# A fused attention and two-MoE kernel: a rewritten order of the instructions of a head pair, 128-row maxima for head 0, and second buffers for the rests of k and q

## The chip, the cores and the metric

The kernel runs on one core of a Trainium2 chip. The metric is the device time of one execution in microseconds (us). The engines are named as the profile names them: PE is TensorE's matmul pipe and PEld its weight loads, DVE is VectorE, ACT is ScalarE, POOL is GpSimd, and SP is SyncE, which only issues DMAs here.

## The reference

Attention over 16 heads (2 batches of 8) with 1152 keys, a head size of 64, and queries averaged in pairs (576 queries per head); then a gated MoE layer; then four experts mixed by `domain_probs`.

```python
q_pool = q.reshape(B, H, S // 2, 2, D).mean(axis=3)
scores = scale * np.matmul(q_pool, k.transpose(0, 1, 3, 2))
attn = np.exp(scores - np.max(scores, axis=-1, keepdims=True))
x = np.matmul(attn / attn.sum(-1, keepdims=True), v)
x = (x @ w_a * (x @ w_b)) @ w_out          # 1152x512 by 512x1536
out = sum(p[:, e] * (np.maximum(x @ w1[e], 0) @ w2[e]) for e in range(4))
```

## The kernel before

**Precision.** Each factor that must be exact is split into a high part (fp32r) and a rest: kh and kl for k, qh and ql for q. The rests of k, of q and the sum qs of the two queries live in the pool `lo`.

**Stages.** Attention takes the first 290 us or so, and what follows it (the two MoE layers) the rest. The heads come in eight pairs; the two heads of a pair lie in the upper and the lower 64 partitions of kq, kh, kl, qh and ql.

**One head.** For each of 9 key tiles a step `qk` writes scores: two matmuls of At (kh over kl) with QHt (qh twice), line 527, and two of Bt (kh and a row of ones) with QLt (ql and the row of negative maxima), line 532. ACT takes the exponential (`e`, line 537; PS has two score buffers). A step `pv` multiplies by V (line 542, four passes). After nine of them `evac` copies the result out on ACT, and the next head's first `pv` writes into the same PSUM banks. The tiles At, Bt, QHt and QLt exist once for even and once for odd heads; they are filled by SBUF-to-SBUF copies that SP issues: `da` (two, from kh and kl), `db` (from kh), `dh` (two, from qh), `dl` (from ql), and the row of maxima (`rm`, `rw`, from mr).

**Maxima.** While pair p is scored, the maxima of pair p+1 are found: 27 steps `mx`, each one matmul of kh with QB (block-diagonal qh, line 417) into one of two PSUM buffers, and one reduction on DVE (line 432). A third `mx` must wait for the first one's reduction. QB is filled by `qb`, two DMAs.

**What sets the order.** It is written out by hand. `FIRST` is the list for heads 0 and 1, `PROG` for a pair (18 steps `qk`: nine for the even head, nine for the odd). Each engine and SP takes its instructions strictly in this order. Other tokens: `k`, `qs`, `qh`, `ql`, `klo0` to `klo2` make the parts of a later pair (casts on ACT, differences on DVE, line 332 for klo); `lq`, `lk0` to `lk2`, `ldf` load q, thirds of k, and v; `nr`, `nb`, `n` normalise the previous pair; `w` is one step of splitting a weight; the last step of a split issues the load of the next weight block (`stg`, 1 MB, line 143). `klo0` writes kl, which `da` of the same pair's odd head reads.

**Head 0** is scored in two column parts, C0 = 256 queries (token `A`, part `a` of the pv) and the other 320 (`C`, `c`), so that it can begin before all of q is there. Its maxima are taken per 128 queries (tiles 0 to 4): tiles 0 to 2 ahead of the token list, tiles 3 and 4 as six tokens `x`; `r1` turns those of the second part into a row. All of them use the upper 64 rows alone (kh with qh). `warm` puts matmuls of zeros in front.

Of the kernel before, what the change touches and what calls it, by code (L numbers as in the profile page):

```python
# [34 lines left out]
STOP = None  # L35
KR = 3
KN = S // KR
WARM = (8, 2, 2)
NE = 8
NORM = ("nr", "nb", "n", "n", "n", "n")  # L40
C0 = 256
C1 = SQ - C0
FIRST = """
A kh1
A x qh1 kl1 x a dh1 ql1 da1 lv1 a x x
A
A x x a a zq a r1 db1 qs a y y k
C
C klo0 y a y a y c y c klo2 y y qh
# [13 lines left out]
""".split()  # L63
FIRST_ONLY = set("A C a c x y r1 R1 E1 E2 qh1 kh1 kl1 ql1 da1 dh1 db1 lv1 zq".split())
PROG = """
qk mx da dh dl db rw
qk mx pv mx
qk mx pv mx pv klo0 lq
qk mx pv mx evac
mx qk mx klo1  # L70
mx qk n pv mx pv ql mx pv
mx qk mx klo2 lk0
mx qk w mx ldf nr pv lk1
mx qk nb mx pv lk2
mx qk mx da dh dl db
mx qk mx pv
mx qk mx
qk mx qs pv n mx pv w pv evac
qk mx k
qk w qh pv ldf n n qb pv rm pv w  # L80
qk w pv
qk
qk n pv n w
""".split()
ENG = {"qs": "V", "qh": "A", "k": "A", "ql": "V", "klo0": "V", "klo1": "V", "klo2": "V", "mult": "V", "xhi": "A", "xlo": "V"}
F64_TINY_BITS = 2.0 ** -15
# [4 lines left out]
def kernel(  # L91
# [139 lines left out]
    with tc.manual_schedule():  # L231
        att = ExitStack()
        kq_p = att.enter_context(tc.tile_pool(name="kq", bufs=2))
        pair_p = att.enter_context(tc.tile_pool(name="pair", bufs=2))
        lo_p = att.enter_context(tc.tile_pool(name="lo", bufs=1))
        b_p = att.enter_context(tc.tile_pool(name="b", bufs=1))
        e_p = att.enter_context(tc.tile_pool(name="e", bufs=NE))
        m_p = att.enter_context(tc.tile_pool(name="m", bufs=2))
# [9 lines left out]
        def psum(kind, base, n, count):  # L248
            i = turn[kind]
            turn[kind] = (i + 1) % count  # L250
            return PS[:, base + i * n:base + (i + 1) * n, :]
# [10 lines left out]
        def rows(i):  # L262
            return slice(64 * i, 64 * i + 64)

        def fill_consts(i, e):
            fill = e.memset
            one = 64 - 64 * i
            fill(QLt[i][rows(1 - i), :].bitcast(F32), 0.0)
            fill(Bt[i][rows(1 - i), :].bitcast(F32), 0.0)
            fill(Bt[i][one:one + 1, :].bitcast(F32), 1.0)  # L270
# [17 lines left out]
        emitted = set()  # L288
# [20 lines left out]
        def load_q(p):  # L309
            q_t[p] = q_p.tile([128, S], F32, tag="q", name="q")  # L310
            nc.sync.dma_start(out=q_t[p], in_=kq[p, :, S:])
# [49 lines left out]
        def own_qh(i, e, cs=slice(0, SQ)):  # L361
            cast(e, QHt[i][rows(i), cs], qs_t[0][rows(i), cs])

        def own_ql(i, e, cs=slice(0, SQ)):
            e.tensor_tensor(
                out=QLt[i][rows(i), cs], in0=qs_t[0][rows(i), cs],
                in1=QHt[i][rows(i), cs].bitcast(F32), op=ALU.subtract,
            )

        def own_kh(i, ks):  # L370
            cast(nc.scalar, At[i][rows(i), ks], kq_t[0][rows(i), ks])
# [37 lines left out]
        def max_mm(out, h, qi, r):  # L409
            p, i = divmod(h, 2)  # L410
            ks = slice(r * KN, (r + 1) * KN)
            if p > 0:
                lhs, rhs = QB[:, qi, :], kh_t[p][:, ks]
            else:
                part = rows(0) if i == 0 else slice(0, 128)
                lhs, rhs = QHt[i][part, qi * 128:min(SQ, (qi + 1) * 128)], At[i][part, ks]
            nc.tensor.matmul(out=out[:lhs.shape[1]], lhsT=lhs, rhs=rhs, start=True, stop=True)  # L417

        def max_slot(h, qi):
            p, i = divmod(h, 2)  # L420
            if p not in m_t:
                m_t[p] = m_p.tile([128, 10, KR], F32, tag="m", name="m")
            return m_t[p][:n_q(h, qi), qi + 5 * i, :]

        def n_q(h, qi):
            return min(128, SQ - 128 * qi) if h < 2 else 128

        def max_step(h, i):
            qi, r = divmod(i, KR)
            mx = psum("mx", 2, 1, 2)[:, 0, :KN]  # L430
            max_mm(mx, h, qi, r)
            nc.vector.tensor_reduce(  # L432
                out=max_slot(h, qi)[:, r:r + 1], in_=mx[:n_q(h, qi)], axis=AX.X, op=ALU.max
            )

        def max_wide(h, qi, base):
            for r in range(KR):
                max_mm(PS[:, base + r, :KN], h, qi, r)
            nc.vector.tensor_reduce(
                out=max_slot(h, qi)[:, 0:1], in_=PS[:, base:base + KR, :KN], axis=AX.XY, op=ALU.max  # L440
            )

        def max_col(p, c, n=KR, parts=128):
            if p not in mc_t:
                mc_t[p] = m_p.tile([128, 10], F32R, tag="mc", name="mc")
            nc.vector.tensor_reduce(
                out=mc_t[p][:parts, c], in_=m_t[p][:parts, c, :n], axis=AX.X, op=ALU.max
            )
# [16 lines left out]
        def row_direct(c):  # L465
            cs, tiles = ((slice(0, C0), range(2)), (slice(C0, SQ), range(2, 5)))[c]
            mx = PS[:, 3, :] if c == 0 else psum("mx", 2, 1, 2)[:, 0, :]
            for qi in tiles:
                n, at = n_q(0, qi), 128 * (qi - tiles[0])
                nc.tensor.matmul(  # L470
                    out=mx[0:1, at:at + n], lhsT=mc_t[0][:n, qi:qi + 1], rhs=nid[:n, :n],
                    start=True, stop=True,
                )
            nc.scalar.activation(
                out=QLt[0][64:65, cs], in_=mx[0:1, :cs.stop - cs.start], func=AF.Copy
            )
# [144 lines left out]
        def warm(n, bank=0):  # L621
            for _ in range(n):
                nc.tensor.matmul(out=PS[:, bank, :], lhsT=Z[:, :128], rhs=Z, start=True, stop=True)
# [5 lines left out]
        nc.vector.memset(Z.bitcast(F32), 0.0)  # L629
        warm(WARM[0])  # L630
        fill_consts(0, nc.gpsimd)
# [30 lines left out]
        own_ql(0, nc.gpsimd, c1)  # L662
        warm(WARM[1], 4)
        row_direct(0)
        max_wide(0, 2, 0)
        load_q(1)
        for r in range(KR):
            load_k(1, r)
# [17 lines left out]
        count = dict.fromkeys("ACacxy", 0)  # L686

        def first(tok):
            n = count.get(tok, 0)
            if tok in count:  # L690
                count[tok] += 1
            if tok in "AC":
                assert tok == "A" or "r1" in emitted
                qk_half(tok == "C", n)
                emitted.update((tok, t) for t in (2 * n, 2 * n + 1))
                if tok == "C" and n == KT // 2:
                    emitted.add(("qk", 0, KT - 1))
            elif tok in "ac":
                assert (tok.upper(), n) in emitted
                pv_half(tok == "c", n)  # L700
                pv_at[0] += tok == "c"
            elif tok == "x":
                assert n < 2 * KR
                max_step(0, 3 * KR + n)
            elif tok == "r1":
                assert count["x"] == 2 * KR
                max_col(0, slice(2, 3), 1)
                max_col(0, slice(3, 4))
                max_col(0, slice(4, 5), KR, 64)
                row_direct(1)  # L710
                emitted.add("r1")
            elif tok == "y":
                assert n < 5 * KR and {"dh1", "da1"} <= emitted
                max_step(1, n)
            elif tok == "R1":
                assert count["y"] == 5 * KR
                max_col(0, slice(5, 9))
                max_col(0, slice(9, 10), KR, 64)
                row_one()
                emitted.add(("row", 1))  # L720
            elif tok in ("E1", "E2"):
                assert count["ac"[tok == "E2"]] == KT
                evac_half(tok == "E2")
                emitted.add(("evac", 0) if tok == "E2" else "E1")
            else:
                need = {"kl1": "kh1", "ql1": "qh1", "dh1": "qh1", "db1": "kh1", "da1": "kl1"}
                assert tok not in need or need[tok] in emitted
                {
                    "qs1": lambda: own_qs(1, nc.gpsimd),
                    "qh1": lambda: own_qh(1, nc.scalar),  # L730
                    "kh1": lambda: own_kh(1, slice(0, S)),
                    "kl1": lambda: [own_klo(1, r, nc.gpsimd) for r in range(KR)],
                    "ql1": lambda: own_ql(1, nc.gpsimd),
                    "da1": lambda: own_put_kl(1, slice(0, S)),
                    "dh1": lambda: own_put_qh(1),
                    "db1": lambda: put(Bt[1][rows(1), :], At[1][rows(1), :]),
                    "lv1": lambda: [fill_v(1, nc.gpsimd), load_v(1)],
                    "zq": lambda: nc.gpsimd.memset(QB.bitcast(F32), 0.0),
                }[tok]()
                emitted.add(tok)  # L740

        for h in range(1, min(NHX, NH)):
# [3 lines left out]
            for tok in FIRST if h == 1 else PROG[half:] if h % 2 else PROG[:half]:  # L746
# [45 lines left out]
                elif tok in ("nr", "nb", "n"):  # L792
                    i = norm_at[0]
                    pr, i = divmod(i, 6)
# [125 lines left out]
        w = W.pop(("ab", 0))  # L920
# [14 lines left out]
        for f in range(1, NF):  # L935
# [3 lines left out]
            w = W.pop(("ab", f))  # L939
# [7 lines left out]
        for d in range(KC):  # L947
            px2 = psum("ps", 0, NTC, 2)
            for hf in range(2):
                w = W.pop(("o", (d, hf)))  # L950
# [115 lines left out]
```

## Time and profile before

| | |
|---|---|
| median of 3 runs | 917.49 us (917.13 to 918.91) |
| profiled execution | 916.18 us, of which the span from first to last instruction is 914.4 us |
| PE busy | 901.8 us (99%) |
| DVE, ACT, POOL busy | 460.9, 273.2, 73.0 us |

The span is what the trace shows; 1.8 us of the profiled execution's time lie around it. PE's ends are modelled, so its busy share says that PE is the engine in front and not that it never waits: two matmul instructions can stand further apart than their work needs. Waits are therefore to be read from the starts of instructions.

### The profile page before, as it was taken

What the parts mean: (1) busy time and instruction counts of PE and PEld (TensorE: products, weight loads), DVE (VectorE), ACT (ScalarE), POOL (GpSimd) and SP (SyncE); (2) the same over time, 40 slices, a digit from 0 to 9 for tenths busy, and PEclk for the clock granted to TensorE, in tenths of its full rate; (3) what the DMA queues carried; (4) which work ended last, traced back from release to release, by engine and by line L of the source; (5) the groups of instructions that cost most, each with busy time, mean ns of one, the idle gap of its engine ahead of it and who ended that gap; (6) DMA issues with size and microseconds to landing.
All of it is one profiled execution on the core that took longest, in us unless ns stands there. A gap on an engine that the chain in (4) does not pass through costs nothing.

```text
span 914.4 us, 11517 instructions
## 1 busy us (share of the span) xinstructions
PE 901.8 (99%) x4707; PEld 818.2 (89%) x4707; DVE 460.9 (50%) x791; ACT 273.2 (30%) x395; POOL 73.0 (8%) x43
## 2 busy tenths in 40 slices
PE   9999999899999999999999999999999999999998
PEld 6778888788888999999999999889988998899986
DVE  5866765666713898888876233113421242124311
ACT  4445445355443333333231132002300131003200
POOL 6000000000000222122322000000000000000000
PEclk9999999999999999999999999999999999999999
DMA  7568568666450221222222022001300121001011
GB/s 179 134 183 192 145 142 192 147 150 156 102 144 0 93 81 62 90 82 70 72 103 93 4 90 92 1 0 47 99 40 1 47 93 47 1 28 65 1 57 47
DMA packets 49385, 76.99 MB, mean 84 GB/s; under 512 B 32496, under 2 KB 36084, under 8 KB 45748
## 3 DMA queue, kind: packets, MB, share of 16 engines
q1 hardware_dynamic: 49332, 76.25, 29.5%
q8 instruction: 37, 0.61, 0.3%
q14 instruction: 16, 0.13, 0.0%
HBM read 51.96 MB, written 2.39 MB: 59 GB/s over the span
## 4 chain that ended last, share of the span: by engine, by line
PE 91%; DVE 4%; DMA 2%; ACT 1%; SPq 1%; issue 1%; DVEq 0%; ACTq 0%
PE PS L885 44%; PE PS L1008 21%; PE PS L542 12%; PE PS L417 5%; PE PS L532 3%; PE PS L527 3%; PE PS L507 1%; DMA A<-kl 1%; SPq L389 1%; DVE m L432 1%; DMA QH<-qh 0%; DMA QL<-ql 0%; DVE R L873 0%; PE PS L497 0%; DVE w L192 0%
## 5 line engine op out<-in xcount | busy, mean ns | idle before, releaser
L885 PE MATMUL PS<-X,w 128*128 128x384 f32 x2016 | 351.7, 334 | 0.6 <-ACT asb L911 0.5
L885 PEld LDWEIGHTS PS<-X,w 128*128 128x128 f32 x2016 | 349.8, 188 | 1.8 <-ACT asb L911 1.3
L1008 PE MATMUL PS<-w,hs 128*128 128x512 f32 x864 | 197.3, 389 | 0.0
L1008 PEld LDWEIGHTS PS<-w,hs 128*128 128x128 f32 x864 | 162.1, 188 | 33.4
L542 PE MATMUL PS<-e,VF 128*128 128x288 f32 x540 | 149.4, 408 | 0.7 <-ACT U L563 0.3
L432 DVE TENSOR_REDUCE m<-PS 128x1 f32<-128x384 f32 (+1 forms) x210 | 113.0, 553 | 69.1 <-PE PS L417 63.2
L981 ACT ACTIVATE hs<-PS 128x1152 fp32r<-128x1152 f32 x32 | 36.3, 1135 | 281.3 <-PE PS L885 281.3
L537 ACT ACTIVATE e<-PS 128x576 f32<-128x576 f32 x135 | 86.3, 650 | 110.0 <-PE PS L532 109.0
L542 PEld LDWEIGHTS PS<-e,VF 128*128 128x128 f32 x540 | 99.2, 190 | 20.4 <-issue 0.9
L982 DVE SCALAR_TENSOR_TENSOR hs<-PS,hs 128x1152 fp32r<-128x1152 f32 x32 | 43.4, 1358 | 134.3 <-ACT hs L981 134.3
L187 POOL TENSOR_TENSOR t<-v,w 128x512 f32<-128x512 f32 (+2 forms) x22 | 57.0, 2591 | 414.6 <-ACT w L177 414.6
L417 PE MATMUL PS<-kh,QB 128*128 128x384 f32 x189 | 78.9, 431 | 5.3 <-DVE m L432 4.8
L1017 DVE SCALAR_TENSOR_TENSOR acc<-PS,p_n,acc 128x512 f32<-128x512 f32 x27 | 20.3, 751 | 115.7 <-PE PS L1008 115.7
L885 PE MATMUL PS<-G,w 128*128 128x384 f32 x432 | 75.0, 334 | 0.0
L885 PEld LDWEIGHTS PS<-G,w 128*128 128x128 f32 x432 | 74.9, 188 | 0.0
L527 PE MATMUL PS<-QH,A 128*128 128x288 f32 x270 | 66.6, 328 | 0.0
L532 PE MATMUL PS<-QL,B 128*128 128x288 f32 x270 | 58.2, 297 | 0.1
L527 PEld LDWEIGHTS PS<-QH,A 128*128 128x128 f32 x270 | 49.3, 190 | 6.0 <-ACT e L537 0.3
L417 PEld LDWEIGHTS PS<-kh,QB 128*128 128x128 f32 x189 | 35.7, 190 | 17.8 <-DVE m L432 13.7
L532 PEld LDWEIGHTS PS<-QL,B 128*128 128x128 f32 x270 | 43.6, 189 | 0.5 <-issue 0.3
L222 DVE TENSOR_TENSOR w<-stg,w 128x1024 fp32r<-128x1024 f32 x32 | 38.9, 1216 | 8.1 <-ACT w L221 8.1
L192 DVE TENSOR_TENSOR w<-t,c 128x512 fp32r<-128x512 f32 (+2 forms) x44 | 39.7, 941 | 1.0
(84 smaller groups left out, 482.7 us busy)
## 6 DMA issues: line engine op xcount, KB each, us to landing
stg<-in_w_dram SPq DMA_DIRECT2D x16, 1024.0 KB
stg<-in_wab_dram SPq DMA_DIRECT2D x12, 1024.0 KB
stg<-in_wout_dram SPq DMA_DIRECT2D x8, 768.0 KB
VF<-in_vo_dram SPq DMA_DIRECT2D x16, 288.0 KB
A<-kl SPq DMA_DIRECT2D x15, 288.0 KB
q<-in_kq_dram SPq DMA_DIRECT2D x7, 576.0 KB
kq<-in_kq_dram SPq DMA_DIRECT2D x21, 192.0 KB
A<-kh SPq DMA_DIRECT2D x14, 288.0 KB
```

Source lines behind the costliest of these rows:

```text
L187: nc.gpsimd.tensor_tensor(out=t, in0=v, in1=h.bitcast(F32), op=ALU.subtract)
L192: nc.vector.tensor_tensor(out=l, in0=t, in1=c, op=ALU.add)
L222: nc.vector.tensor_tensor(out=t[:, 1, :n], in0=s, in1=t[:, 0, :n].bitcast(F32), op=ALU.subtract)
L417: nc.tensor.matmul(out=out[:lhs.shape[1]], lhsT=lhs, rhs=rhs, start=True, stop=True)
L432: nc.vector.tensor_reduce(out=max_slot(h, qi)[:, r:r + 1], in_=mx[:n_q(h, qi)], axis=AX.X, op=ALU.max)
L527: nc.tensor.matmul(out=st[:, c, :HQ], lhsT=At[i][:, ks], rhs=QHt[i][:, c * HQ:(c + 1) * HQ], start=True, stop=False,)
L532: nc.tensor.matmul(out=st[:, c, :HQ], lhsT=Bt[i][:, ks], rhs=QLt[i][:, c * HQ:(c + 1) * HQ], start=False, stop=True,)
L537: nc.scalar.activation(out=e, in_=st[:, :, :HQ], func=AF.Exp, scale=1.0 / 16.0)
L542: nc.tensor.matmul(out=PS[:, c, :HQ], lhsT=VFt[h % 2][:, t, :], rhs=e[:, c, :], start=(t == 0), stop=(t == KT - 1),)
L885: nc.tensor.matmul(out=ps[n], lhsT=wt(kc)[:, wi, w0:w0 + 128], rhs=src(kc)[:, xi, n * TOK:(n + 1) * TOK], start=(kc == first and i == 0), ...
L982: nc.vector.scalar_tensor_tensor(out=gv(hs[:, 1, :]), in0=ph[:, :, :TOK], scalar=0.0, in1=gv(hs[:, 0, :].bitcast(F32)), op0=ALU.max, op1=A ...
L1008: nc.tensor.matmul(out=po, lhsT=cur[f][:, hi, ts], rhs=wv[:, wi, cs], start=(f == 0 and i == 0), stop=(f == NFE - 1 and i == 2),)
```

## The change

PROG is rewritten: the same tokens stand in other places. Three lines of FIRST change, `warm` has four matmuls instead of two at its second place, the maxima of head 0's tile 2 move from ahead of the list into it (nine `x` instead of six), and maxima of tiles 2 to 4 contract over all 128 rows. Pool `lo` gets two buffers for each of kl, qs and ql.

```diff
-WARM = (8, 2, 2)
+WARM = (8, 4, 2)
 FIRST = """
-A kh1
-A x qh1 kl1 x a dh1 ql1 da1 lv1 a x x
-A
+A kh1 x x
+A x qh1 kl1 x dh1 ql1 da1 x
+A x lv1 a x a
 A x x a a zq a r1 db1 qs a y y k
...
 PROG = """
-qk mx da dh dl db rw
+dh mx mx rw
+qk
+qk n mx dl db mx pv pv da klo0 mx
...
-        lo_p = att.enter_context(tc.tile_pool(name="lo", bufs=1))
+        lo_p = att.enter_context(tc.tile_pool(name="lo", bufs=2))
...
-                part = rows(0) if i == 0 else slice(0, 128)
+                part = rows(0) if i == 0 and qi < 2 else slice(0, 128)
...
         row_direct(0)
-        max_wide(0, 2, 0)
         load_q(1)
...
             elif tok == "x":
-                assert n < 2 * KR
-                max_step(0, 3 * KR + n)
+                assert n < 3 * KR and ("A", 0) in emitted
+                max_step(0, 2 * KR + n)
             elif tok == "r1":
-                assert count["x"] == 2 * KR
-                max_col(0, slice(2, 3), 1)
-                max_col(0, slice(3, 4))
+                assert count["x"] == 3 * KR
+                max_col(0, slice(2, 4))
                 max_col(0, slice(4, 5), KR, 64)
```

What moves is seen in each engine's list of instructions. Line numbers grow by one from the rewritten table on (417 becomes 418). First PE at the start of head 0, before, from the maxima's row of the first part (nid, mc) on; in square brackets stand the semaphores that a row waits for (DMAHW are landings of DMAs).

```order
L470 MATMUL PS<-nid,mc 1x128 [waits DVE_49,Activation_49]
L470 MATMUL PS<-nid,mc 1x128
L417 MATMUL PS<-A_110,QH_114 128x384 [waits Activation_49]
L417 MATMUL PS<-A_110,QH_114 128x384 x2
L497 MATMUL PS<-QH_114,A_110 128x256 [waits DMAHW6_49,DMAHW0_49]
L498 MATMUL PS<-QL_116,B_112 128x256 [waits Activation_49,Pool_49]
```

And the same place in the changed kernel.

```order
L471 MATMUL PS<-nid,mc 1x128
L498 MATMUL PS<-QH_114,A_110 128x256 [waits DMAHW6_49,DMAHW0_49]
L499 MATMUL PS<-QL_116,B_112 128x256 [waits Activation_49,Pool_49]
L498 MATMUL PS<-QH_114,A_110 128x256
L499 MATMUL PS<-QL_116,B_112 128x256
L418 MATMUL PS<-A_110,QH_114 128x384 [waits DMAHW5_49]
L418 MATMUL PS<-A_110,QH_114 128x384 [waits DMAHW1_49]
```

The three maxima of tile 2 stood ahead of the scores and waited for ACT's cast alone; they now follow the first two score tiles, and the first of them waits for a DMA, the copy of the second part of qh into the lower 64 rows (`own_put_qh(0, c1)`, the fourteenth DMA that SP issues).

Next PE at the start of an even head of a steady pair, before, behind the odd head's last `pv`.

```order
L527 MATMUL PS<-QH_114,A_110 128x288 x2
L532 MATMUL PS<-QL_116,B_112 128x288 x2
L417 MATMUL PS<-kh,QB 128x384
L527 MATMUL PS<-QH_114,A_110 128x288 x2
L532 MATMUL PS<-QL_116,B_112 128x288 x2
L417 MATMUL PS<-kh,QB 128x384
L542 MATMUL PS<-e,VF_119 128x288 x2
L417 MATMUL PS<-kh,QB 128x384
```

And now.

```order
L418 MATMUL PS<-kh,QB 128x384 x2
L528 MATMUL PS<-QH_114,A_110 128x288 x2
L533 MATMUL PS<-QL_116,B_112 128x288 x2
L528 MATMUL PS<-QH_114,A_110 128x288 x2
L533 MATMUL PS<-QL_116,B_112 128x288 x2
L418 MATMUL PS<-kh,QB 128x384 x2
L543 MATMUL PS<-e,VF_119 128x288 x4
L418 MATMUL PS<-kh,QB 128x384
```

Two maxima stand ahead of the head's first score step and therefore read QB earlier; the even head has 18 of the 27 maxima instead of 19, and more of them stand between two `pv`.

Last SP in the odd head, before (R and rd belong to the normalisation, kq are thirds of k).

```order
L581 DMA rd<-rc 128x9
L317 DMA kq<-in_kq_dram 128x384
L586 DMA R<-rd 64x576 x2
L317 DMA kq<-in_kq_dram 128x384
L389 DMA A_110<-kh 64x1152
L389 DMA A_110<-kl 64x1152
L389 DMA QH_114<-qh 64x576 x2
L389 DMA QL_116<-ql 64x576
L389 DMA B_112<-kh 64x1152
```

And now.

```order
L582 DMA rd<-rc 128x9
L587 DMA R<-rd 64x576 x2
L390 DMA QL_116<-ql 64x576
L318 DMA kq<-in_kq_dram 128x384
L390 DMA QH_114<-qh 64x576 x2
L318 DMA kq<-in_kq_dram 128x384
L390 DMA A_110<-kh 64x1152
L390 DMA A_110<-kl 64x1152
L390 DMA B_112<-kh 64x1152
```

The last third of k now comes behind R, the copies of ql and the two of qh, and the copies into At come near the end.

## Rows read from the trace of the kernel before

**Rows 1.** The page: PE in its list of engines (busy us, share, instructions).

```profile
PE 901.8 (99%) x4707; PEld 818.2 (89%) x4707; DVE 460.9 (50%) x791; ACT 273.2 (30%) x395; POOL 73.0 (8%) x43
```

**Rows 2.** Windows: stretch, length, busy (x) of PE, PEld, DVE, ACT, POOL; clock, DMA, GB/s.

```profile
55.66:71.49 15.83, 15.31 (x81) 12.73 (x80) 11.50 (x24) 7.02 (x11) 0.00 (x0) 1.00 0.95 283
...
86.49:104.27 17.78, 17.75 (x94) 15.14 (x93) 12.43 (x26) 7.92 (x14) 0.74 (x1) 1.00 0.57 136
104.27:119.26 14.99, 14.99 (x82) 12.82 (x82) 10.13 (x26) 9.19 (x16) 0.00 (x0) 1.00 0.79 176
119.26:137.62 18.36, 18.19 (x94) 15.19 (x92) 12.38 (x26) 7.31 (x12) 0.00 (x0) 1.00 0.56 133
...
152.62:175.11 22.49, 19.29 (x94) 16.32 (x93) 12.12 (x26) 7.95 (x14) 0.00 (x0) 0.92 0.65 155
...
190.10:208.56 18.46, 18.03 (x94) 15.18 (x92) 12.81 (x27) 7.31 (x12) 0.00 (x0) 1.00 0.56 132
```

**Rows 3.** Chain of waits, 97 to 117 us: start, length, what.

```profile
97.36 0.97 PE PS L542 x4
98.33 0.17 PE PS L417
...
100.19 0.56 PE PS L417 x2
```

**Rows 4.** Timeline, 149 to 172 us (start, length, instruction, idle before and releaser).

```profile
151.59 0.40 SPq L143 DMA_DIRECT2D stg<-in_wab_dram  x1
...
152.66 0.59 SPq L389 DMA_DIRECT2D A<-kl  x1
...
162.53 0.56 DVE L332 TENSOR_TENSOR kl<-kq,kh 128x384 fp32r<-128x384 f32 x1 [4.33 <-DMA A<-kl]
...
163.61 0.44 PE L417 MATMUL PS<-kh,QB 128*128 128x384 f32 x1 [3.20 <-DVE m L432]
```

**Rows 5.** Window behind that wait: the granted clock stands before the DMA share.

```profile
164.00:168.00 4.00, 4.00 (x16) 3.50 (x15) 2.07 (x5) 1.30 (x2) 0.00 (x0) 0.57 0.77 204
```

**Rows 6.** Groups by line: the reductions of the maxima on DVE (busy us, mean ns).

```profile
L432 DVE TENSOR_REDUCE m<-PS 128x1 f32<-128x384 f32 x204 | 110.0, 553 | 67.0 <-PE PS L417 61.1
```

**Rows 7.** Timeline, 0 to 62 us: the start of head 0.

```profile
9.23 0.59 SPq L654 DMA_DIRECT2D kq<-in_kq_dram  x1
...
9.80 1.32 PE L417 MATMUL PS<-A,QH 64*128 64x384 f32 x3
...
9.91 0.55 SPq L389 DMA_DIRECT2D QH<-QH  x1
...
11.06 0.58 PE L497 MATMUL PS<-QH,A 128*128 128x256 f32 x1
...
14.33 1.16 ACT L282 ACTIVATE A<-kq 64x1152 fp32r<-64x1152 f32 x1 [1.41 <-DMA kq<-in_kq_dram]
...
21.49 0.59 PE L470 MATMUL PS<-nid,mc 128*1 128x128 f32 x3
```

**Rows 8.** Chain of waits, 9 to 24 us: score matmuls of 256 and of 320 columns.

```profile
11.64 0.21 PE PS L498
...
23.21 0.15 PE PS L498
```

**Rows 9.** Timeline, 104 to 121 us: odd head 5 and what follows.

```profile
106.37 1.34 SPq L317 DMA_DIRECT2D kq<-in_kq_dram  x1
...
113.03 1.16 ACT L282 ACTIVATE kh<-kq 128x1152 fp32r<-128x1152 f32 x1
...
115.32 1.31 SPq L389 DMA_DIRECT2D QB<-qh  x2
...
120.39 0.34 PE L417 MATMUL PS<-kh,QB 128*128 128x384 f32 x1
```

**Rows 10.** Chain of waits, 97 to 117 us: two copies from issue to landing.

```profile
108.98 4.04 DMA QH<-qh
...
116.72 3.18 DMA QL<-mr
```

More of the change, by code (lines that the diff above doesn't have):

```diff
@@ L65 @@
 PROG = """
-qk mx da dh dl db rw
[L67 to L81, printed above, removed]
-qk
-qk n pv n w
+dh mx mx rw
+qk
+qk n mx dl db mx pv pv da klo0 mx
+qk mx pv
+qk mx pv evac mx
+qk lq klo1
+qk mx mx pv mx pv ql mx ldf mx pv mx
+qk klo2 lk0 mx
+qk mx nr pv mx mx nb pv
+qk w
+qk mx dl lk1 mx pv qs mx dh
+qk mx lk2 pv da w mx
+qk mx db pv n mx n
+qk pv mx evac k mx
+qk w qh
+qk qb n pv rm pv ldf
+qk pv n pv w
+qk
+qk w n pv w
 """.split()
```

## The prediction

> **What bounds the kernel now.** I read the page first. PE is busy 99% of the span [rows 1], so the engine in front is clear; what can be won is only where PE's list stands still, or where it runs at the lower clock. The page cannot show how much that is, because a matmul that stands in the queue counts as busy. So I next cut attention into heads at the first score matmul of each and asked for the length of each stretch [rows 2]. The odd heads are the measure: head 5 takes 14.99 us, and the six odd heads from 3 to 13 all take 14.99 or 15.00, busy from end to end. An even head of a steady pair does the same work with 19 maxima instead of 8. A maxima matmul that nobody holds up costs 0.17 us [rows 3], so an even head should take 14.99 + 11 x 0.17 = 16.86. The reader is to see how far the even heads lie above that: head 4 takes 17.78 (0.92 over, and head 12 prints the same length), head 6 18.36 (1.50), head 10 18.46 (1.60), head 8 22.49 (5.63). Head 2 has three `pv` steps fewer, of 0.97 us each [rows 3], and should take 13.95; it takes 15.83 (1.88 over). The sum for these six is 12.4 us. The pair of heads 14 and 15 has no maxima, and I expect nothing there.
>
> Why they lie above it, two views say. Ordinary even heads: two adjacent maxima that should take 0.35 us take 0.56 [rows 3], and a reduction on DVE takes 553 ns [rows 6]. There are two PSUM buffers, so where three maxima stand with less than 0.55 us of other work for each, PE goes at DVE's pace. Head 8: the timeline shows DVE idle 4.33 us ahead of a kl difference until a copy out of kl into At had landed; that copy was issued at 152.66, right behind a 1 MB weight load of 151.59, and PE waited 3.20 us for the maxima that stood behind the difference on DVE [rows 4]. Behind that wait the granted clock is 0.57 over 4 us, between its two levels of 1.2 and 2.4 GHz [rows 5], which costs another 0.43 x 4 = 1.7. These two make 4.9 of head 8's 5.63.
>
> **The change, part by part.** *Second buffers.* kl gets another buffer, so `klo0` no longer waits for the copies of its own pair but for those of the pair before, a whole pair (33 us) old. The wait of 3.20 and the 1.7 of low clock go: 4.9 us. What is late next? The weight load still delays everything behind it on SP's queue: the copy into At took until DVE's start at 162.53 [rows 4], 10 us after the head's start. Its reader is now only the odd head, at 152.62 + 16.9 = 169.5. In the new list SP issues `da` behind `dh`, `rw`, `dl` and `db`; the bytes ahead of it are then those that were behind it, and I allow 3 us more, 165.5: still 4 us early.
>
> *The order of the pair.* The maxima are spread. I walked through the new list at 0.17 for a maximum, 0.97 for a `pv`, 0.53 for a score step (the rest of an odd head: 14.99 less nine `pv` and eight maxima, by nine), and 0.55 on DVE for each reduction and each difference. The densest place in the even head is one score step, six maxima and three `pv`: 4.5 us of PE against 4.1 on DVE (six reductions and the 0.75 us of `ql`). The first four steps of the odd head hold 7.5 us of PE and about 7.1 of DVE. PE comes out ahead of DVE nowhere by much, so the 0.7 to 1.9 us over in each even head should shrink to a few tenths. Bounds: nothing left gives 12.4 saved; half of the ordinary excess (12.4 - 4.9 = 7.5) left gives 8.6. I take 0.25 us left in each of six pairs, near the good end because no place of the walk is over its share: 12.4 - 1.5 = 10.9 saved.
>
> *What the even head's start now needs.* Two maxima stand ahead of the first score step, so QB must have landed some 0.5 us sooner than before. QB is issued when qh is cast, at 115.32 in head 5, and the next maximum stood at 120.39 [rows 9]; its list, not QB, held it. The two QB copies take 3.2 to 4.0 us by the nearest rows [rows 10], the second being issued 0.6 later: 119.1 to 120.0, where 119.26 will now be asked. On the other side the cast of kh, which precedes qh on ACT, is moved forward by a score step, and the load of v no longer stands ahead of QB on SP. But the last third of k, which that cast reads, is issued later: before, at 106.37, 2.1 us into the odd head; now behind R, `dl`, a third of k and the two of `dh`, about 5 us into it. With 3.2 to 4.0 us to land it comes at 8.2 to 9.0, where the cast (at 113.03, 8.8 into the head, before [rows 9]) could start at about 8.1. So QB is between on time and 0.9 us late; behind the waiting maximum stand the whole next head's scores. My 0.25 holds a part of that; the bad end is 0.9 x 6 = 5.4.
>
> *Head 0.* Before, the three maxima of tile 2 ran from 9.80 to the first score matmul at 11.06 [rows 7], on the upper 64 rows, as soon as qh was cast. Now the scores come first (they can start at about 10.4, when the kl copy is there), and then the first `x` reads all 128 rows, for which SP's copy of qh must have landed. That copy is issued at 9.91, right behind a load of k of 9.23, whose landing ACT waits for until 14.33 [rows 7]. On the same queue the copy cannot be there much before that: I take 14.5. So PE, with 0.9 us of scores, stands still from 11.4 to 14.5, and everything behind it in PE's list waits: the next scores, their exponentials, `a`, and the row of maxima (`r1`) at 21.49. From 11.06 to 21.49 lie 10.4 us of work; the three moved maxima add 1.3, the scores already done take 0.9 off: 10.8 us are left at 14.5.
>
> These are at the low clock. A score matmul of 256 columns takes 0.21 us at 11.64, which is 1.2 GHz, and one of 320 takes 0.15 at 23.21, about 2.2 columns a ns, the full level [rows 8]; the spacing changes close to 20.8, though PE had hardly paused since 9.5. If it changes there again, `r1` comes at 20.8 + (14.5 + 10.8 - 20.8) / 2 = 23.1, which is 1.6 us late. Ends: full level at once from 14.5 gives 14.5 + 5.4 = 19.9, 1.6 early; the low one throughout gives 25.3, 3.8 late. I take 1.6 late, as the nearest row has it. After `r1` FIRST is as before and the delay passes through.
>
> The pause deserves a second look. The row shows that a pause of 3.20 us was followed by the lower clock [rows 4, 5]. The Trainium skill, TensorE: Matmul & The Clock Gate, section "Why this matters for your kernels", warns of just that: gaps between bursts of matmuls bring the half clock back. By that rule the new pause of 3.1 us speaks against this change: the sum would take the bad end, 3.8, in place of 1.6. The trace agrees that a pause of that length was followed by a fall; no run here shows a pause while the clock is still low. That case is rival E.
>
> *The rest.* The two more zero matmuls fill a time in which PE waits for the row's maxima anyway (until 9.5): nothing, and if that cover were gone, two of 0.43. `row_mm`, `rw`, `ldf` and the norm steps keep their number. The MoE stages are untouched and merely start sooner.
>
> **The sum.** 10.9 saved, 1.6 given back: 9.3. The profiled execution at 916.18 becomes 906.9; it stands 1.3 below the median of the runs, so against 917.49 I forecast 908.2.
>
> **The rivals.**
> *A. Head 0 costs nothing.* The denser 128-row work brings the full clock by 18 or so. For it: the low level before went with 64-row maxima, short pauses and few columns. Against it: nothing shows what raised it. Then `r1` is at 18 + (25.3 - 18) / 2 = 21.7, and the time 917.49 - 10.9 + 0.2 = 906.8; with all of the gain, 905.
> *B. QB takes the place of DVE.* With 0.9 us in each of six pairs on top, it is 908.2 + 5.4 = 913.6.
> *C. Slower than before,* by the same chain: the last third of k -> cast of kh -> qh -> QB -> first maximum. It gains the upper hand when QB is more than 9.3 / 6 = 1.6 us late in each pair. At 2.5 us late it would be 908.2 + 15 = 923. For it speaks a copy that took 10 us behind a weight load [rows 4]; against it, that such loads stand in only a few pairs, and the ordinary copies take 3 to 4 us.
> *D. The second buffer does not do what it says:* DVE meets another late landing in head 8 (the gathered denominators, `dc`, share that queue). Then 4.9 stays: 913.1. Against it, `nr`, which reads them, comes 14 us into the head.
>
> *E. Head 0 at the low clock to `r1`,* because of the new pause: 917.49 - 10.9 + 3.8 = 910.4. For it: the fall behind the pause of head 8. Against it: 10.8 us of work without a pause follow, and in head 8 the level was back after less than 4.
>
> **How the numbers follow.** My forecast has 0.53, A 0.15, E 0.08, B 0.10, D 0.06, C 0.04, and 0.04 is for what I have not seen. Without B and C, head 0's two ends and the two ends of the saving give 904 to 912; with B, 913.6. The range that leaves out two in ten is 904.5 to 912.5. Within 0.2%, about what a measurement of this kernel can tell from no change, is 915.7 to 919.3: it needs B at its worst or D with the bad end of head 0, 0.05. Slower is C and part of the unseen, 0.04. Faster is 0.91.
>
> **What would show it.** Right: heads 4, 6, 8, 10 and 12 all near 16.7 to 17.0 us and head 8 without a low clock; no wait of DVE for a copy out of kl; PE idle from about 11.4 to 14.5, ended by the DMA of qh; `r1` near 23. Wrong: a wait of PE's first maximum of a pair for QB, of ACT's cast for kq, or head 0 ending its first part before 22 us. The prediction is most exposed in QB's landing and in the clock of head 0.

## The result and the profile after

| | before | after |
|---|---|---|
| median | 918.00 us (917.13 to 918.91, 4 runs) | 908.62 us (907.51 to 909.75, 4 runs) |
| profiled execution | 916.18 us, span 914.4 | 909.75 us, span 908.0 |

The ratio is 0.9898, with a 95% interval from 0.9881 to 0.9915; 908.2 was forecast. The profiled execution after is the longest of its four, and the one before lay below its median, so the two traces differ by 6.4 us where the medians differ by 9.4. In a second comparison of the same two kernels, on another occasion, the medians were 917.45 and 909.92, a ratio of 0.9921 (0.9903 to 0.9939).

All of the 6.4 us lies ahead of the first MoE layer: the stretch from its first matmul to the end takes 626.0 us in both traces. PE on the page, against [rows 1]:

```profile
PE 893.5 (98%) x4709; PEld 816.6 (90%) x4709; DVE 459.1 (51%) x792; ACT 270.8 (30%) x395; POOL 72.1 (8%) x43
```

The windows of heads 2 to 6, 8 and 10, divided as in [rows 2]. A stretch begins at a head's first score matmul, and two maxima now stand ahead of it, so an even stretch holds 16 maxima and an odd one 11. By the prediction's measure (14.99 for an odd head with 8, 0.17 for each maximum) that makes 16.35 and 15.50 us.

```profile
57.31:71.19 13.88, 13.84 (x77) 12.06 (x77) 10.19 (x20) 6.16 (x10) 0.00 (x0) 1.00 0.88 269
71.19:89.98 18.79, 16.60 (x86) 13.45 (x85) 10.87 (x28) 9.54 (x17) 0.00 (x0) 1.00 0.67 167
89.98:106.35 16.37, 16.37 (x89) 14.34 (x89) 12.09 (x26) 6.27 (x10) 0.00 (x0) 1.00 0.69 158
106.35:122.99 16.64, 15.78 (x87) 13.45 (x85) 10.06 (x25) 10.37 (x19) 0.73 (x1) 1.00 0.59 147
122.99:139.37 16.38, 16.38 (x90) 14.35 (x90) 12.15 (x26) 6.28 (x10) 0.00 (x0) 1.00 0.68 159
154.88:171.25 16.37, 16.37 (x89) 14.34 (x89) 12.09 (x26) 6.51 (x11) 0.00 (x0) 1.00 0.88 221
186.74:203.12 16.38, 16.38 (x89) 14.35 (x89) 12.11 (x26) 6.50 (x11) 0.74 (x1) 1.00 0.66 158
```

The even heads, which held the whole loss before, are busy from end to end, head 8 among them (22.49 before), at the full clock. What is new stands in the odd heads: head 3 is 3.29 over and head 5 1.14. The timeline of head 3 says where (start, length, instruction, idle before and releaser):

```profile
71.78 0.33 SPq L582 DMA_DIRECT2D rd<-rc  x1
74.74 1.11 SPq L587 DMA_DIRECT2D R<-rd  x2
...
78.51 0.59 SPq L318 DMA_DIRECT2D kq<-in_kq_dram  x1
...
78.73 0.46 DVE L597 TENSOR_TENSOR U<-U,R 128x288 f32<-128x288 f32 x1 [1.30 <-DMA R<-rd]
...
83.28 1.16 ACT L283 ACTIVATE kh<-kq 128x1152 fp32r<-128x1152 f32 x1 [2.53 <-DMA A<-kh]
84.35 0.63 ACT L538 ACTIVATE e<-PS 128x576 f32<-128x576 f32 x1
...
85.03 0.53 PE L528 MATMUL PS<-QH,A 128*128 128x288 f32 x2 [1.77 <-ACT e L538]
```

Read it upwards. PE waits 1.77 us for an exponential, to free a score buffer. The exponential stands on ACT behind the cast of kh, and that cast waited 2.53 us. The releaser named is a copy into At, but that copy reads the kh of another pair than the cast writes. What the cast reads is kq, whose last third was issued at 78.51; by the trace's semaphore updates it had landed at 83.12, 4.61 us later and 0.16 us before the cast. It was issued so late because SP takes its list in order: R must wait for rd to land, from 71.78 to 74.74, and the rest of SP's list stands behind R. In this head rd itself came late, 0.59 us into the head; in heads 5, 7, 9 and 11 it was issued 1.7 us ahead of the head's start. It waited for the gathered denominators (`dc`), a copy that took 6.97 us to land behind two 1 MB weight loads of head 2. Head 5 shows the rest of the chain again:

```profile
104.65 0.33 SPq L582 DMA_DIRECT2D rd<-rc  x1
108.11 1.11 SPq L587 DMA_DIRECT2D R<-rd  x2
...
111.70 0.59 SPq L318 DMA_DIRECT2D kq<-in_kq_dram  x1
...
116.28 1.16 ACT L283 ACTIVATE kh<-kq 128x1152 fp32r<-128x1152 f32 x1 [1.87 <-DMA kq<-in_kq_dram]
```

PE then waits 0.86 us for an exponential. The Trainium skill, DMA: Bandwidth & Descriptors, section "Anatomy of one DMA — SWDGE (gpsimd) path", says of DMA engines in general that they do not wait for semaphores: such a wait happens on the issuing sequencer, before the transfer is handed on. SP's rows agree: R stands 2.96 us behind rd in head 3 and 3.46 in head 5.

Head 0, PE's timeline, against [rows 7]:

```profile
10.33 0.58 PE L498 MATMUL PS<-QH,A 128*128 128x256 f32 x1 [0.34 <-DMA A<-kl]
...
14.61 1.01 PE L418 MATMUL PS<-A,QH 128*128 128x384 f32 x2 [3.06 <-DMA QH<-QH]
...
20.92 0.28 PE L498 MATMUL PS<-QH,A 128*128 128x256 f32 x1
...
22.66 0.54 PE L471 MATMUL PS<-nid,mc 128*1 128x128 f32 x3
```

The pause and its releaser are as predicted, to 0.2 us; `r1` is 1.17 us later than before. The clock column prints 1.00 for this part of head 0 in this trace and in that of the kernel before, although 0.21 us for 256 columns is the pace of 1.2 GHz; in a repeat of the changed kernel, at the same pace, it prints 0.50. For head 0 of these two traces the level is therefore read from the spacing.

### The profile page after: what moved, and what is told of

Read it like the earlier page. It is cut to its first block, busy times and chain, and to the rows that moved or that the text cites. A ratio compares the mean times of both kernels' runs of the same rounds, so it can differ in the third digit from the quotient of the medians.

```text
span 908.0 us, 11502 instructions
## 1 busy us (share of the span) xinstructions
PE 893.5 (98%) x4709; PEld 816.6 (90%) x4709; DVE 459.1 (51%) x792; ACT 270.8 (30%) x395; POOL 72.1 (8%) x43
## 4 chain that ended last, share of the span: by engine, by line
PE 91%; DMA 3%; DVE 3%; ACT 1%; SPq 1%; issue 1%; ACTq 0%; DVEq 0%
PE PS L884 44%; PE PS L1007 22%; PE PS L543 12%; PE PS L418 4%; PE PS L528 3%; PE PS L533 3%; PE PS L508 1%; DMA kq<-in_kq_dram 1%; DMA dc<-D 1%; DMA B<-kh 1%; DMA QH<-QH 1%; DMA A<-kh 0%; DVE R L872 0%; SPq L390 0%; DMA rd<-rc 0%
## 5 line engine op out<-in xcount | busy, mean ns | idle before, releaser
L538 ACT ACTIVATE e<-PS 128x576 f32<-128x576 f32 x135 | 84.4, 648 | 108.0 <-PE PS L533 107.2
L418 PE MATMUL PS<-kh,QB 128*128 128x384 f32 x189 | 72.7, 425 | 1.5 <-DVE m L433 1.1
```

The costliest lines, as they stand in the source:

```text
L538: nc.scalar.activation(out=e, in_=st[:, :, :HQ], func=AF.Exp, scale=1.0 / 16.0)
```

## The experiments

**The second buffers alone**, on the kernel before.

```diff
-        lo_p = att.enter_context(tc.tile_pool(name="lo", bufs=1))
+        lo_p = att.enter_context(tc.tile_pool(name="lo", bufs=2))
```

> The kernel before with two buffers for kl, qs and ql and nothing else. My theory: the wait of 3.20 us in head 8 and the low clock behind it go, 4.9 us, and nothing else: 918.0 - 4.9 = 913.1, with heads 4, 6, 10 and 12 as long as before (17.8 to 18.5). Rival, that the buffer is the whole of the gain: 908 to 909. Rival, that another late landing takes the wait's place in head 8: 916 to 918.

Measured: 913.18 us against 916.48 for before in the same comparison, 0.9958 (0.9939 to 0.9977), so 3.3 us less; the interval reaches from 2.1 to 5.6 us and holds the 4.9 of the theory. Head 8's window:

```profile
152.94:170.87 17.93, 17.91 (x94) 15.12 (x92) 12.12 (x26) 7.96 (x14) 0.00 (x0) 1.00 0.84 193
```

It falls from 22.49 to 17.93, by 4.56, and every other even head stays within 0.2 of its length before. The wait of 3.20 and the low clock behind it belonged to the single buffer.

**The new order with one buffer**: the same line, put back in the changed kernel.

> The changed kernel with one buffer for kl, qs and ql as before. In the new list the copy of kl into At is issued some 3 us later in the even head than before, and the kl difference of the next pair stands only about 3 us into it: the copy lands about 8 us into the head (97.8 in head 4, which begins at 89.4). My theory: DVE waits about 5 us in each of six even heads, PE some 4 of them, 24 to 26 us, and up to 1.7 more for each where the clock falls: 933 to 945. Rival, that the buffer matters in head 8 alone and the order does the rest: 908.6 + 4.9 = 913.5.

Measured: 938.97 us, 1.0240 (1.0215 to 1.0266), as the theory had it. Windows of heads 4 and 8, three rows of its waits (us, times, longest), and the timeline in head 4:

```profile
93.76:114.39 20.63, 18.00 (x90) 15.51 (x90) 12.00 (x26) 6.28 (x10) 0.00 (x0) 0.92 0.52 121
...
166.92:191.79 24.87, 18.88 (x89) 16.39 (x89) 12.00 (x26) 6.62 (x11) 0.00 (x0) 0.86 0.56 145
```

```profile
DVE kl L333 <- DMA A<-kl: 24.0, 4, 8.3
PE PS L418 <- DVE m L433: 23.8, 9, 6.0
...
DVE kl L333 <- issue: 10.9, 2, 5.5
```

```profile
101.20 0.56 DVE L333 TENSOR_TENSOR kl<-kq,kh 128x384 fp32r<-128x384 f32 x1 [4.97 <-DMA A<-kl]
...
102.28 0.69 PE L418 MATMUL PS<-kh,QB 128*128 128x384 f32 x1 [2.63 <-DVE m L433]
```

The new list issues the copies into At later, so `klo0` finds its buffer taken in every pair, not in one: DVE waits six times ahead of it, four times put down to the copy and twice to "issue". All six even heads are longer than in the change, by 3.3 to 8.5 us, and in five of them the clock falls as well (0.84 to 0.92 over the window; head 10 keeps 1.00). The two parts do not add: -3.3 alone and +22.5 alone (with the new head 0) make -7.5 to -9.4 together.

**Head 0 as before**, in the changed kernel: FIRST, WARM, the maxima ahead of the list and the 64 rows.

```diff
-WARM = (8, 4, 2)
+WARM = (8, 2, 2)
...
-                part = rows(0) if i == 0 and qi < 2 else slice(0, 128)
+                part = rows(0) if i == 0 else slice(0, 128)
...
+        max_wide(0, 2, 0)
```

> The changed kernel with head 0 as before: its lists, the zero matmuls, 64-row maxima, tile 2 ahead of the scores. My theory: the pause of 3.1 us at 11.5 goes, the row of the second part's maxima comes at 21.5 in place of 22.7, and the time is 1.2 us shorter: 907.4. Rival, that the 128-row maxima bring the full clock sooner and so pay for the pause: no shorter, or longer by up to 1.

**The new order of head 0 with maxima on 64 rows**: the `part` line alone, put back.

> The changed kernel with maxima of head 0 on 64 rows again, in the new places. The first of them then does not wait for the copy of qh. My theory: no pause at 11.5, the row of maxima at 20.5 to 21.5, 907 to 907.6. Rival, that 64 rows hold the clock low longer: the full level comes later than 20.2 (24 or so), and the gain of the pause is lost: 908.5 to 910.

Measured: 909.84 us, 0.9920 (0.9893 to 0.9948), and 909.89 us, 0.9924 (0.9901 to 0.9947). Neither is clear of the change (0.9898 and 0.9921): both theories missed, and the outcome is nearer to the rivals. Their windows around the change of level, the first kernel's and then the second's; the granted clock stands before the DMA share:

```profile
21.00:23.00 2.00, 2.00 (x7) 1.26 (x5) 0.63 (x1) 0.00 (x0) 0.26 (x1) 0.50 1.14 268
23.00:25.00 2.00, 2.00 (x14) 1.81 (x13) 0.92 (x2) 1.70 (x3) 0.00 (x0) 0.99 0.81 249
```

```profile
19.00:21.00 2.00, 2.00 (x7) 1.23 (x7) 0.60 (x2) 0.60 (x1) 1.94 (x3) 0.50 0.71 148
21.00:23.00 2.00, 2.00 (x9) 1.42 (x8) 1.26 (x4) 0.00 (x0) 0.41 (x1) 0.70 1.13 264
```

`r1` came at 22.34 and at 22.59 us, against 22.66 in the change and 22.34 in its repeat; head 1's first score step came at 39.50 and 38.28, against 38.29 and 37.98. Without the pause PE had done more work by 14.6, but it stayed at 1.2 GHz until 23.0 and, in the second kernel, until 22.2 (0.70 over the window is the full level for 0.8 of 2 us). In these traces the lower level took what the pause would have taken. So head 0's part of the change is not shown to cost anything against its own undoing. That 64 rows are the reason for the later rise is not shown either: the four traces with 64 rows rose at 20.8, 21.2, 22.2 and 23.0 us, the four with 128 rows and the changed kernel's head 0 at 19.4 to 20.2, but those four have the pause as well.

**A repeat, and two mends**, run together with before at 917.45. The repeat is the changed kernel unaltered.

> The changed kernel once more, beside the next three and the kernel before on one chip: 8 to 10 us below the kernel before. Its profile shows whether the waits of heads 3 and 5 (3.3 and 1.1 us in the first profile) are there in each execution: with a landing that varies, 1 to 5 us in the odd heads together.

*The last two thirds of k earlier*: both loads go from the odd head into the seventh score step of the even head, ahead of R.

```diff
-qk klo2 lk0 mx
+qk klo2 lk0 lk1 lk2 mx
...
-qk mx dl lk1 mx pv qs mx dh
-qk mx lk2 pv da w mx
+qk mx dl mx pv qs mx dh
+qk mx pv da w mx
```

> The changed kernel with the second and the last third of k (lk1, lk2) issued behind the first, two score steps before the even head's end, ahead of rd, R and the copies of ql and qh on SP's queue. My theory: ACT's cast of kh no longer waits for them, and heads 3 and 5 lose what they are over 15.5 us: 2 to 4.4 us less than the changed kernel in the same job. Rival, that R lands later by the same bytes and DVE's multiplication by R, or the copies for the next even head, become the wait: no gain, with a wait of DVE for R in every odd head.

*Head 0's pause filled*: all four `A` and one `a` stand ahead of the first `x`.

```diff
-A kh1 x x
-A x qh1 kl1 x dh1 ql1 da1 x
-A x lv1 a x a
-A x x a a zq a r1 db1 qs a y y k
+A
+A
+A a kh1
+A qh1 kl1 x x a dh1 x x a ql1 da1 x x lv1 a x x a x zq r1 db1 qs a y y k
```

> The changed kernel with four score steps and the first pv of head 0 ahead of its first x, so that PE has 4.4 us of work at the low clock from 10.3 on, while the copy of qh is on its way. My theory: the pause of 3.1 us shrinks to less than 0.5, and the row of the second part's maxima comes at 19.5 to 21 in place of 22.6: 1.5 to 3 us less than the changed kernel in the same job. Rival, that DVE, with nine reductions of 0.55 us that can now only begin at 15, sets the row's time: less than 1 us.

*Both.*

> Both of these edits. If their waits are apart, as I hold, the gains add: 3.5 to 7 us less than the changed kernel in the same job, 901.5 to 905. Rival, that head 0's gain only moves the same waits for DMAs forward, so that less than the sum is left.

| | median | ratio to before |
|---|---|---|
| repeat | 909.92 | 0.9921 (0.9903 to 0.9939) |
| k early | 906.63 | 0.9885 (0.9868 to 0.9901) |
| pause filled | 906.85 | 0.9890 (0.9872 to 0.9908) |
| both | 905.21 | 0.9873 (0.9855 to 0.9891) |

Odd heads 3, 5, 9 and 11 of the repeat, and the same with k early:

```profile
70.96:87.95 16.99, 15.77 (x87) 13.36 (x86) 9.83 (x25) 9.55 (x17) 0.00 (x0) 1.00 0.65 162
104.33:120.03 15.70, 15.70 (x86) 13.41 (x85) 9.98 (x25) 10.38 (x19) 0.73 (x1) 1.00 0.66 156
168.26:186.87 18.61, 16.11 (x86) 13.51 (x85) 11.42 (x30) 9.30 (x17) 0.00 (x0) 1.00 0.55 133
203.24:218.75 15.51, 15.51 (x86) 13.52 (x85) 10.16 (x26) 9.77 (x17) 0.00 (x0) 1.00 0.66 171
```

```profile
70.84:88.15 17.31, 16.33 (x86) 13.51 (x85) 10.71 (x28) 9.55 (x17) 0.00 (x0) 1.00 0.73 173
104.51:120.02 15.51, 15.51 (x86) 13.52 (x85) 9.95 (x25) 10.38 (x19) 0.73 (x1) 1.00 0.64 147
168.27:183.78 15.51, 15.51 (x86) 13.52 (x85) 10.13 (x26) 9.52 (x17) 0.00 (x0) 1.00 0.64 147
200.15:215.66 15.51, 15.51 (x87) 13.52 (x85) 10.15 (x26) 9.77 (x17) 0.00 (x0) 1.00 0.64 147
```

The repeat is 7.5 us below the kernel before, where 8 to 10 was expected. The lost time is again in odd heads, 4.8 us (1.49, 0.20 and 3.11), but in head 9 instead of head 5: the place changes from one execution to the next, the mechanism (cast of kh, then exponentials, then PE) does not. The size changes too: in the two kernels with another head 0 and the same order of the pair it is 2.4 and 2.7 us. With the loads ahead of R heads 5, 9 and 11 stand at 15.51, and 3.3 us are saved, as the theory had it. Head 3 keeps 1.81.

With the pause filled the time is 3.1 us shorter than the repeat's, the upper end of what was expected, and `r1` comes at 20.30. With both, the saving is 4.7 us where the two alone make 6.4. The medians leave room for either, but the traces say why. With the pause filled alone, head 1's first score step came 1.46 us sooner than in the repeat (36.52 against 37.98); the odd heads lost 3.05 us in place of 4.80, although nothing in them had been changed. That second part is the spread of the late landings and not the filled pause. With both, 1.59 us come from head 0 and 3.1 from the odd heads: 4.7. Small waits take the pause's place: PE in head 0, with both.

```profile
14.54 0.62 PE L418 MATMUL PS<-A,QH 128*128 128x384 f32 x2 [0.87 <-DMA QH<-QH]
...
19.99 0.40 PE L471 MATMUL PS<-nid,mc 128*1 128x128 f32 x3 [0.71 <-DVE mc L447]
...
21.68 0.59 PE L418 MATMUL PS<-A,QH 128*128 128x384 f32 x2 [0.66 <-DMA A<-kl]
```

**What is left in head 3.** R lands late there (DVE's 1.30 in the timeline above), and reductions stand behind the multiplication by R. The kernel with both, and the first two normalisation steps of the odd head moved behind the last reduction, beside a repeat of the kernel with both:

```diff
-qk mx db pv n mx n
-qk pv mx evac k mx
+qk mx db pv mx
+qk pv mx evac k mx n n
```

> The kernel with both mended orders, and in the odd head the first two multiplications by R stand one step later, behind the last reduction of the maxima. Theory: what is left in head 3 (1.7 to 1.9 us over 15.5) is DVE standing still for R, whose landing is late in the first pair alone, with the reductions of the maxima queued behind it; with the reductions ahead of it head 3 takes 15.5 to 15.8 us and the time falls by 1.3 to 1.7, to about 903.7. Rival: head 3 is held by something else that is late with it, and stays at 17 or more; the time is that of the kernel with both, 905.2 (within 0.7).

> The kernel with both mended orders once more, to stand beside the one with the later multiplications on the same chip: 905.2 within 0.7, head 3 at 17 to 17.5 us with DVE's wait for R.

Measured: 906.03 us (0.9883, 0.9864 to 0.9903) and, a little more than expected for the repeat, 906.01 us (0.9881, 0.9860 to 0.9902). Heads 3 and 7, first with the later steps, then the repeat, and PE at the start of head 8 with the later steps:

```profile
70.70:86.70 16.00, 15.75 (x86) 13.43 (x85) 9.99 (x26) 9.65 (x17) 0.00 (x0) 1.00 0.72 174
134.96:152.09 17.13, 15.78 (x87) 13.43 (x86) 10.32 (x26) 10.26 (x19) 0.88 (x1) 1.00 0.63 142
```

```profile
69.36:86.67 17.31, 16.34 (x87) 13.51 (x86) 10.74 (x28) 9.54 (x17) 0.00 (x0) 1.00 0.75 176
134.94:151.46 16.52, 15.77 (x87) 13.43 (x86) 10.30 (x26) 10.25 (x19) 0.73 (x1) 1.00 0.67 148
```

```profile
145.69 0.67 ACT L283 ACTIVATE qh<-qs 128x576 fp32r<-128x576 f32 x1
146.39 1.31 SPq L390 DMA_DIRECT2D QB<-qh  x2
...
151.63 0.61 PE L418 MATMUL PS<-kh,QB 128*128 128x384 f32 x2 [1.35 <-DMA QB<-qh]
```

Head 3 goes most of the way that the theory said (17.31 to 16.00, where 15.5 to 15.8 was expected), but the time does not fall. In this execution head 7 gives back 0.61: the cast of qh stands 0.58 later in the head, so does QB, and the first maximum of the next pair waits for it, 1.35 against 0.75 in the repeat. The rest lies ahead of head 1, whose first score step came at 37.72 against 36.43: 1.29 us, 0.91 of them one more wait for QB, and none of the moved instructions stands ahead of it. The three add up to the 0.6 us by which this span is the longer one. So the theory holds for head 3 and fails for the time. Why head 0 was slower in this execution, and whether it was in the others, is open.

## Why the prediction was right, step by step

**The second buffer: right.** 4.9 was worked out for head 8; with the buffer alone its window became 4.56 shorter, and the waits of DVE for the copy of kl are gone after.

**The even heads: right, and better than forecast.** 16.37 plus the two maxima that left the stretch (0.35) is 16.72, inside the 16.7 to 17.0 that was to show it. The six even heads stand 0.6 over in all (head 2 0.44, the others 0.02 or 0.03), where 1.5 was allowed. Saved there: 12.4 - 0.6 = 11.8, not 10.9. (The walk's score step comes out at 0.54 and not at 0.53; nothing turns on it.)

**The odd heads: the step that failed.** "What the even head's start now needs" saw that the last third of k would be late, and put it at the same place in every pair: issued "about 5 us" into the odd head, landed at 8.2 to 9.0. In the trace it landed 8.0, 8.6 and 7.5 us into heads 7, 9 and 11, which lose nothing, but 11.9 us into head 3 and 9.8 into head 5. What varies, and what the step held fixed, is R's wait. R waited for rd for 1.5 to 1.7 us in heads 7, 9 and 11, but for 2.96 and 3.46 in heads 3 and 5 (and rd itself was late in head 3), so that the load was issued 7.32 and 5.35 us into these two and 3.4 to 3.6 into the others. Its landing took 3.9 to 5.2 us in the five heads, where 3.2 to 4.0 was taken. Why rd lands later in some pairs than in others is open. The step also looked for the damage at the wrong exit: rival B had it go through qh and QB to the next pair's first maximum, 0.9 us in each pair. PE waited for QB in neither trace of the changed kernel; the delay went through ACT's own list instead, where the exponentials stand behind the waiting cast. That cast was named as a sign of error, but not what stands behind it, and the sum has no term for it. The price was 4.4 us in one trace and 4.8 in the other, in two or three heads; of head 3's part about 1.3 is R, going by the last experiment. QB is next in line all the same: PE waited for it in the last two traces, for 2.5 us in three waits with the later steps and for 0.7 in one without.

**Head 0: right in place, near in size.** PE's pause was 11.55 to 14.61, and `r1` at 22.66 stands for 23.1: 1.17 late for 1.6. The level changed a little earlier than taken: 0.21 us for 256 columns up to 18.6, 0.12 from 20.8 on. Rival E (the low level up to `r1`) did not come about, though the pause it rests on did. Rival A did not either. Rival D is out by the window of head 8, C by the result. What raises the level was not known to the prediction and is not known now. It took over the row of the kernel before, and that was near enough, though no run shows why it should be.

**The sum.** In the traces 11.8 saved, less 4.4, less about 1.3 for head 0 and its aftermath in head 1, is 6.1, against 6.4 between the spans. No trace shows the other 3 us of the first comparison's 9.4; the trace of the changed kernel is the longest of its four executions. The forecast of 9.3 lies between the two measured differences of medians, 9.4 and 7.5. It came out well in part by luck: the error in the odd heads was offset by even heads and a head 0 that were better than allowed; on the second comparison the saving is 1.8 less than forecast.

## What to carry to other kernels

When loads are moved behind a transfer that must wait, add that wait to each of them, at its longest and not at its usual length, and then read what stands behind their reader on its own engine, before following the data to the next engine. A buffer and an order have to be judged as one change: here each is worth something else without the other. When one wait is removed from a list this full, look for the next transfer in line before counting the gain.

## What was not expected of the hardware

In head 0 the clock is not set by the instructions alone. The kernel with the filled pause and the kernel with both have the same list in head 0 and the same stop of 0.21 us, and yet, first the one, then the other:

```profile
11.81 0.58 PE L498 MATMUL PS<-QH,A 128*128 128x256 f32 x1 [0.21 <-ACT e L502]
...
12.40 0.41 PE L498 MATMUL PS<-QH,A 128*128 128x256 f32 x1
```

```profile
11.78 0.39 PE L498 MATMUL PS<-QH,A 128*128 128x256 f32 x1 [0.21 <-ACT e L502]
...
12.12 0.28 PE L498 MATMUL PS<-QH,A 128*128 128x256 f32 x1
```

In the first the level falls to 1.2 GHz at that point (granted 0.50 from 13 to 15 us), in the second it stays at 2.4 (1.00). The repeat of the kernel with both, unaltered, has the same stop of 0.21 us and falls as well (0.50 from 13 to 15 us). Over the twelve traces the last rise in head 0 came between 6.2 and 23.0 us. Single runs of the kernel before spread from 913.5 to 920.8 us; how much of that is the clock of head 0 is not shown. What decides it is open.
